# Engine lists ordered with changes of the PE array's tiling counted, and denser fill products in planned gaps

## The chip, the cores and the metric

The kernel runs on one core of a Trainium2 chip. The metric is the device time of one execution in microseconds (us), the median over several runs. Five engines work side by side, each through its own list of instructions in order: PE (TensorE, matmul), ACT (ScalarE), DVE (VectorE), POOL (GpSimd) and SP (SyncE, which here only issues DMA transfers). They wait for one another through semaphores.

## What is computed

The reference, cut to what matters (batch 8, 8 heads, 576 rows of width 64, 32 packed rows, d_ff 2048):

```python
def sm_attn(qq, kk, vv):
    s = scale * np.matmul(qq, kk.transpose(0, 1, 3, 2))
    a = softmax(s)
    return np.matmul(a, vv)
p_packed = sm_attn(p, k, v)             # 32 packed rows attend to 576 rows
out = sm_attn(q, p_packed, p_packed)    # 576 rows attend to the 32 packed ones
x = out.transpose(0, 2, 1, 3).reshape(4608, 512)
h = x @ w_in                            # 512 -> 2048
g = h * (1.0 / (1.0 + np.exp(-beta * h)))
return g @ w_out                        # 2048 -> 512
```

All inputs and the output are float32; the kernel computes its products in bf16.

## The kernel before

Each of the eight batches is one unit of work `b`. 512 of its 576 rows are the main part, the other 64 the "rest", and two batches share one 128-row tile for the last product of the rests.

Attention of a batch: k and q are transposed (by PE for the first two batches, tasks `tr` and `trr`; by DMA from batch 2 on), the scores of the packed rows are products of k and p (`s1`, `s1r`), their exponentials are summed (`z1`) and multiplied with v (`pun`), and DVE normalizes the result to `pp`. Then `s2` makes the scores of the q rows, and `z2` the sums over them. Instead of multiplying the second attention's output with w_in, the kernel first multiplies `pp` with w_in (`w`, product tiles `w_ps`; DVE scales them with beta to `W_bf`), so that one product of `W_bf` with the attention weights `A2T` gives the hidden layer (`h`, sixteen per batch; `hr` for the rests). ACT applies silu (`g`), and the last product (`o`, or for the main part of batches 2 to 7 the seven products `p`/`P` of a Strassen-like scheme with sums `S`, `T4`) goes to the output. The tasks `take`, `add` and `R..` read the product tiles, and `store` writes them out.

`s2` and `w` use the PE array as eight 64x32 tiles at once (eight matmuls with a tile position each, called a burst below); `z1` uses it as two 128x64 tiles. Everything else uses the whole 128x128 array. In the profile all products stand at line 380 (the helper `mm`) and all PE transposes at line 385 (`tp`), so they are told apart by their tiles: `w_ps<-w_in_bf,pp` is `w`, `s_ps<-qT,pp` and `s2r_ps` are the two parts of `s2`, `z_ps<-E1T,ones` is `z1`, `h_ps` is `h`, `pT_ps<-identr,p_dup` is `p_tr`.

The packed rows p of batches 2 to 7 are loaded once (`("ld", "p")`, 384 KB). Two copies, `("p_dup", 0)` and `("p_dup", 1)`, double them into one bf16 tile (line 1168), PE transposes that tile in two halves (`("p_tr", 0)` and `("p_tr", 1)`), each of which reads both copies, and the tasks `pT1` place the result, which the `s1` of batches 2 to 7 read.

The order of every engine's work is written out: `SEQUENCE` holds one list of tasks per engine. `Planner.run` walks the lists, each in its order, with the costs of its tasks (the number or table handed to `task`), and emits the instructions. It emits them in the order of the lists whatever the costs say; two things depend on its times: where ACT's table loads stand in the program, and the fill products. `begin` gives the earliest start of an engine's next task, and `fill` puts fill products (`keep_warm`: 128x128 products of the identity, tile `o_ps<-identr`) into PE's list where `begin` finds a gap before the next task, as long as the time is before `WARM_UNTIL = 60.0` and an output bank is free. A loose task (a conversion) can stand in the list of any of the engines that its cost table names, and the engine is the one in whose list it stands.

PSUM tiles come from rings: four banks `att` for attention and `w` products, two `h`, two `o`. A task that takes a bank waits until the one that held it has been read.

Of the kernel before, what the change touches and what calls it, by code (L numbers as in the profile page):

```python
# [37 lines left out]
WARM_US = 0.3  # L38
# [5 lines left out]
HALVED = (0,)  # L44
PORT = ("S", "T4", "A2", "cast", "w_in", "w_out", "p_dup", "p0_bf")
# [8 lines left out]
        ("brow", 0), ("tr", 0, "k", 0), ("p0_tr", 0), ("brow", 1), ("tr", 0, "k", 1), ("tr", 0, "q", 0),  # L54
        ("trr", 0, "k"), ("brow", 2), ("s1r", 0), ("s1", 0, 0), ("s1", 0, 1), ("brow", 3), ("tr", 0, "q", 1),
        ("p0_tr", 1), ("z1", 0), ("pun", 0, 0), ("pun", 0), ("bcol",), ("s2", 0, 0), ("z2", 0, 0), ("z2", 0, 1),
        ("w", 0, 0), ("w", 0, 1), ("h", 0, 3), ("h", 0, 0), ("tr", 1, "k", 0), ("h", 0, 2), ("h", 0, 1),
        ("tr", 1, "k", 1), ("h", 0, 4), ("o", 0, 0, 1), ("o", 0, 1, 1), ("h", 0, 7), ("h", 0, 6), ("trr", 0, "q"),
        ("w", 0, 2), ("trr", 1, "k"), ("h", 0, 5), ("o", 0, 1, 3), ("o", 0, 0, 3), ("s1r", 1), ("s1", 1, 0),
        ("h", 0, 8), ("h", 0, 9), ("o", 0, 0, 5), ("o", 0, 1, 5), ("s1", 1, 1), ("o", 0, 0, 7), ("o", 0, 1, 7),  # L60
        ("h", 0, 11), ("o", 0, 2, 1), ("w", 0, 3), ("z1", 1), ("o", 0, 2, 3), ("tr", 1, "q", 0), ("o", 0, 2, 5),
        ("h", 0, 10), ("h", 0, 12), ("o", 0, 3, 1), ("h", 0, 14), ("pun", 1, 0), ("o", 0, 2, 7), ("pun", 1),
        ("h", 0, 15), ("h", 0, 13), ("tr", 1, "q", 1), ("o", 0, 3, 3), ("s2", 0, 1), ("o", 0, 3, 5), ("s2", 1, 0),
        ("o", 0, 3, 7), ("w", 1, 0), ("o", 0, 1, 9), ("o", 0, 1, 11), ("o", 0, 0, 9), ("z2", 1, 0), ("o", 0, 0, 11),
        ("z2", 0, 2), ("o", 0, 1, 13), ("trr", 1, "q"), ("o", 0, 1, 15), ("z2", 1, 1), ("o", 0, 0, 13), ("s2", 1, 1),
        ("o", 0, 0, 15), ("o", 0, 2, 9), ("o", 0, 2, 11), ("o", 0, 2, 13), ("z2", 1, 2), ("w", 1, 1), ("o", 0, 3, 9),
        ("o", 0, 3, 11), ("w", 1, 2), ("h", 1, 1), ("h", 1, 3), ("o", 0, 3, 13), ("o", 0, 3, 15), ("h", 1, 0),
        ("w", 1, 3), ("h", 1, 2), ("o", 0, 2, 15), ("p_tr", 0), ("h", 1, 10), ("h", 1, 5), ("p_tr", 1), ("h", 1, 4),
        ("o", 1, 0, 1), ("h", 1, 9), ("o", 1, 1, 1), ("h", 1, 6), ("o", 1, 1, 3), ("h", 1, 8), ("o", 1, 0, 3),
        ("h", 1, 11), ("o", 1, 1, 5), ("h", 1, 7), ("hr", 0, 0), ("o", 1, 0, 5), ("o", 1, 1, 7), ("s1r", 2),  # L70
        ("s1", 2, 1), ("s1", 2, 0), ("o", 1, 1, 9), ("o", 1, 0, 7), ("o", 1, 0, 9), ("hr", 0, 1), ("o", 1, 0, 11),
        ("z1", 2), ("pun", 2, 0), ("pun", 2), ("h", 1, 15), ("o", 1, 1, 11), ("h", 1, 12), ("hr", 1, 0), ("w", 2, 0),
        ("h", 1, 14), ("w", 2, 1), ("h", 1, 13), ("hr", 1, 1), ("w", 2, 2), ("o", 1, 0, 13), ("o", 1, 0, 15),
        ("o", 1, 1, 13), ("o", 1, 1, 15), ("s2", 2, 0), ("o", 1, 2, 1), ("o", 1, 2, 3), ("o", 1, 2, 5), ("z2", 2, 0),
        ("o", 1, 3, 1), ("z2", 2, 1), ("o", 1, 2, 7), ("o", 1, 3, 3), ("o", 1, 2, 9), ("o", 1, 2, 11), ("s2", 2, 1),
        ("o", 1, 2, 13), ("o", 1, 2, 15), ("o", 1, 3, 5), ("o", 1, 3, 7), ("h", 2, 0), ("h", 2, 6), ("s1r", 3),
        ("s1", 3, 1), ("s1", 3, 0), ("o", 1, 4, 1), ("h", 2, 1), ("o", 1, 3, 9), ("z2", 2, 2), ("o", 1, 3, 11),
        ("h", 2, 5), ("o", 1, 4, 3), ("o", 1, 3, 13), ("o", 1, 4, 5), ("o", 1, 4, 7), ("o", 1, 3, 15), ("z1", 3),
        ("w", 2, 3), ("o", 1, 4, 9), ("o", 1, 4, 11), ("h", 2, 7), ("h", 2, 2), ("pun", 3, 0), ("pun", 3),
        ("h", 2, 10), ("o", 1, 4, 13), ("h", 2, 3), ("o", 1, 4, 15), ("h", 2, 8), ("w", 3, 0), ("h", 2, 15),  # L80
        ("w", 3, 1), ("h", 2, 14), ("p", 2, 1, 0), ("h", 2, 11), ("w", 3, 2), ("h", 2, 12), ("p", 2, 1, 1),
        ("h", 2, 4), ("h", 2, 13), ("w", 3, 3), ("h", 2, 9), ("p", 2, 1, 2), ("P", 2, 1), ("hr", 2, 0),
        ("p", 2, 2, 0), ("hr", 2, 1), ("p", 2, 2, 1), ("s2", 3, 0), ("p", 2, 2, 2), ("P", 2, 2), ("s2", 3, 1),
        ("p", 2, 6, 0), ("p", 2, 6, 1), ("z2", 3, 0), ("p", 2, 5, 0), ("z2", 3, 1), ("p", 2, 5, 1), ("p", 2, 6, 2),
        ("P", 2, 6), ("s1r", 4), ("z2", 3, 2), ("s1", 4, 1), ("p", 2, 5, 2), ("s1", 4, 0), ("P", 2, 5),
        ("p", 2, 7, 0), ("p", 2, 7, 1), ("p", 2, 7, 2), ("p", 2, 3, 0), ("p", 2, 3, 1), ("h", 3, 15), ("p", 2, 3, 2),
        ("P", 2, 7), ("h", 3, 14), ("h", 3, 1), ("z1", 4), ("pun", 4, 0), ("h", 3, 8), ("pun", 4), ("h", 3, 7),
        ("p", 2, 4, 0), ("h", 3, 0), ("p", 2, 4, 1), ("h", 3, 9), ("P", 2, 3), ("h", 3, 2), ("p", 2, 4, 2),
        ("h", 3, 5), ("w", 4, 0), ("h", 3, 3), ("w", 4, 1), ("h", 3, 11), ("P", 2, 4), ("h", 3, 10), ("w", 4, 2),
        ("h", 3, 4), ("p", 3, 1, 0), ("h", 3, 13), ("h", 3, 6), ("p", 3, 1, 1), ("w", 4, 3), ("h", 3, 12),  # L90
        ("hr", 3, 0), ("p", 3, 1, 2), ("P", 3, 1), ("p", 3, 2, 0), ("s2", 4, 0), ("p", 3, 2, 1), ("p", 3, 2, 2),
        ("P", 3, 2), ("hr", 3, 1), ("z2", 4, 0), ("s2", 4, 1), ("z2", 4, 1), ("p", 3, 6, 0), ("p", 3, 6, 1),
        ("p", 3, 6, 2), ("z2", 4, 2), ("p", 3, 5, 0), ("P", 3, 6), ("p", 3, 5, 1), ("p", 3, 5, 2), ("s1r", 5),
        ("s1", 5, 1), ("p", 3, 7, 0), ("s1", 5, 0), ("p", 3, 7, 1), ("P", 3, 5), ("p", 3, 7, 2), ("P", 3, 7),
        ("h", 4, 13), ("z1", 5), ("p", 3, 3, 0), ("pun", 5, 0), ("pun", 5), ("h", 4, 0), ("h", 4, 8), ("p", 3, 3, 1),
        ("p", 3, 3, 2), ("h", 4, 15), ("h", 4, 2), ("p", 3, 4, 0), ("p", 3, 4, 1), ("h", 4, 10), ("h", 4, 7),
        ("w", 5, 0), ("p", 3, 4, 2), ("h", 4, 11), ("h", 4, 9), ("w", 5, 1), ("P", 3, 3), ("h", 4, 5), ("h", 4, 1),
        ("P", 3, 4), ("w", 5, 2), ("h", 4, 14), ("h", 4, 3), ("w", 5, 3), ("o", 3, 4, 1), ("h", 4, 4), ("h", 4, 6),
        ("o", 3, 4, 3), ("o", 3, 4, 5), ("hr", 4, 0), ("o", 3, 4, 7), ("h", 4, 12), ("o", 3, 4, 9), ("s2", 5, 0),
        ("o", 3, 4, 11), ("o", 3, 4, 13), ("p", 4, 1, 0), ("o", 3, 4, 15), ("p", 4, 1, 1), ("z2", 5, 0),  # L100
        ("p", 4, 1, 2), ("z2", 5, 1), ("s2", 5, 1), ("P", 4, 1), ("hr", 4, 1), ("p", 4, 2, 0), ("p", 4, 2, 1),
        ("p", 4, 2, 2), ("p", 4, 6, 0), ("P", 4, 2), ("p", 4, 6, 1), ("p", 4, 6, 2), ("h", 5, 7), ("h", 5, 11),
        ("p", 4, 5, 0), ("p", 4, 5, 1), ("h", 5, 3), ("h", 5, 13), ("P", 4, 6), ("p", 4, 5, 2), ("h", 5, 1),
        ("z2", 5, 2), ("h", 5, 10), ("s1r", 6), ("s1", 6, 1), ("P", 4, 5), ("p", 4, 7, 0), ("p", 4, 7, 1),
        ("s1", 6, 0), ("p", 4, 7, 2), ("h", 5, 15), ("h", 5, 8), ("p", 4, 3, 0), ("P", 4, 7), ("p", 4, 3, 1),
        ("p", 4, 3, 2), ("P", 4, 3), ("z1", 6), ("pun", 6, 0), ("pun", 6), ("h", 5, 5), ("p", 4, 4, 0), ("h", 5, 9),
        ("p", 4, 4, 1), ("h", 5, 0), ("w", 6, 0), ("hr", 5, 0), ("w", 6, 1), ("h", 5, 14), ("p", 4, 4, 2),
        ("h", 5, 4), ("w", 6, 2), ("h", 5, 2), ("P", 4, 4), ("h", 5, 12), ("w", 6, 3), ("h", 5, 6), ("p", 5, 1, 0),
        ("hr", 5, 1), ("p", 5, 1, 1), ("s2", 6, 0), ("p", 5, 1, 2), ("P", 5, 1), ("p", 5, 2, 0), ("p", 5, 2, 1),
        ("p", 5, 2, 2), ("P", 5, 2), ("z2", 6, 0), ("p", 5, 6, 0), ("s2", 6, 1), ("z2", 6, 1), ("p", 5, 6, 1),  # L110
        ("p", 5, 6, 2), ("P", 5, 6), ("p", 5, 5, 0), ("s1r", 7), ("s1", 7, 0), ("s1", 7, 1), ("p", 5, 5, 1),
        ("z2", 6, 2), ("p", 5, 5, 2), ("P", 5, 5), ("p", 5, 7, 0), ("h", 6, 8), ("h", 6, 14), ("z1", 7),
# [148 lines left out]
class Planner:  # L261
# [14 lines left out]
    def run(self):  # L276
# [3 lines left out]
        free, done = dict(FROM), {e: 0 for e in todo}  # L280
        freed = {}
        held = {"DVE": 0.0, "POOL": 0.0}
        flight, mode, pipe = [], "exp", 0.0

        def begin(e):
            if done[e] == len(todo[e]):
                return None
            t, at = todo[e][done[e]], free[e]
            if e == "ACT" and t.table not in (None, mode):
                at += TABLE_US  # L290
# [1049 lines left out]
```

## Time and profile before

| | us |
|---|---|
| median of 6 runs | 251.63 |
| lowest and highest of them | 251.26, 252.65 |
| the profiled execution's own time | 251.31 |
| its span, first to last instruction | 249.5 |
| PE busy | 235.7 (94%), 2335 matmuls |
| ACT busy | 174.6 (70%) |
| DVE busy | 154.9 (62%) |
| POOL busy | 62.9 (25%) |
| DMA moved | 54.11 MB |

The costliest groups on PE are `h` (256 matmuls, 72.9 us busy) and the parts of the last product (`o_ps<-...`). Because a matmul's recorded duration overlaps with the next one, the busy sums are too high a measure of the array's work; the distance between two starts is the better one. A group in the profile reads: line, engine, operation, output<-inputs, shapes, count, then busy time, mean ns of one, and the idle time just before with what ended most of it. In the timeline the first two columns are the start in us from the span's beginning and the duration of the merged group.

### The profile page before, as it was taken

How to read it: one execution, taken by the hardware profiler on the slowest of the kernel's cores; microseconds unless marked ns; L12 is line 12 of the kernel's file. 1: busy time of each engine (PE TensorE's matmuls, PEld its weight loads, DVE VectorE, ACT ScalarE, POOL GpSimd, SP SyncE). 2: the span in 40 equal slices, each digit the busy share in tenths (PEclk: the TensorE clock that was granted, in tenths of full speed). 3: DMA queues.
4: the chain of work that ended last, by engine and by line, in shares of the span. 5: the costliest groups of instructions: out<-in, count | busy, mean ns of one | idle time of the engine just before them, and what ended most of it. 6: DMA issues, size and time to landing. Idle time of an engine off the chain costs nothing.

```text
span 249.5 us, 5622 instructions
## 1 busy us (share of the span) xinstructions
PE 235.7 (94%) x2335; PEld 148.0 (59%) x2335; DVE 154.9 (62%) x236; ACT 174.6 (70%) x313; POOL 62.9 (25%) x74
## 2 busy tenths in 40 slices
PE   2985999999999999999999999999999999999992
PEld 1972444433564444686578645776587646767970
DVE  5464768988927536884587475844878356723721
ACT  2385789767797887887688767877797659766110
POOL 8312002006742074055501541523305000000000
PEclk9996599999999999999999999999999999999999
DMA  6999999999999999999499999798491631004122
GB/s 198 302 335 334 336 371 313 350 265 280 160 290 193 301 307 298 244 296 301 112 253 242 327 197 282 177 319 183 92 293 31 117 148 45 1 3 168 45 86 82
DMA packets 74825, 54.11 MB, mean 217 GB/s; under 512 B 42688, under 2 KB 68304, under 8 KB 74800
## 3 DMA queue, kind: packets, MB, share of 16 engines
q1 hardware_dynamic: 74496, 53.68, 80.5%
q8 instruction: 18, 0.29, 0.5%
q10 hardware_dynamic: 304, 0.07, 0.2%
q14 instruction: 7, 0.06, 0.1%
HBM read 37.23 MB, written 9.44 MB: 187 GB/s over the span
## 4 chain that ended last, share of the span: by engine, by line
PE 77%; DMA 16%; POOL 2%; SPq 1%; ACT 1%; DVE 1%; issue 0%; POOLq 0%
PE o_ps L380 42%; PE h_ps L380 21%; DMA k<-in_k_dram 13%; PE w_ps L380 3%; PE hr_ps L380 3%; DMA v<-in_v_dram 3%; PE z_ps L380 2%; PE s_ps L380 2%; PE pp_ps L380 2%; POOL k_bf L461 1%; SPq L440 1%; PE kT_ps L385 1%; ACT L395 1%; SPq L1251 0%; ACT E1T L583 0%; POOL p_dup L1168 0%
## 5 line engine op out<-in xcount | busy, mean ns | idle before, releaser
L823 ACT ACTIVATE g_main<-h_ps 128x512 bf16<-128x512 f32 x128 | 72.7, 596 | 34.6 <-PE h_ps L380 34.5
L380 PE MATMUL h_ps<-A2T,W_bf 128*128 128x512 bf16 x256 | 72.9, 388 | 0.5 <-DVE A2T L733 0.5
L380 PEld LDWEIGHTS <-g_main 128*128 128x128 bf16 x608 | 56.7, 98 | 28.0 <-issue 3.5
L380 PE MATMUL o_ps<-w_out_bf,g_main 128*128 128x256 bf16 (+1 forms) x416 | 72.7, 306 | 0.2 <-DVE o_sb L888 0.2
L792 DVE TENSOR_TENSOR W_bf<-w_ps,beta_bc 128x512 bf16<-128x512 f32 x64 | 41.4, 683 | 17.8 <-PE w_ps L380 17.5
L380 PEld LDWEIGHTS <-W_bf 128*128 128x128 bf16 x512 | 32.5, 99 | 21.8 <-issue 6.6
L395 ACT ACT_TABLE_LOAD x24 | 30.8, 1283 | 1.1 <-PEq L1324 0.7
L380 PE MATMUL o_ps<-w_sum,g_main 128*128 128x256 bf16 x192 | 26.5, 273 | 0.0
L380 PE MATMUL o_ps<-w_sum,g_sum 128*128 128x256 bf16 x192 | 24.7, 273 | 0.0
L461 POOL CAST q_bf<-q 128x1024 bf16<-128x1024 f32 x14 | 16.8, 1206 | 29.5 <-DMA q<-in_q_dram 28.2
L1039 DVE TENSOR_TENSOR o_sb<-o_ps,o_sb 128x512 f32<-128x512 f32 x18 | 12.4, 686 | 16.6 <-PE o_ps L380 15.6
L461 POOL CAST v_bf<-v 128x1024 bf16<-128x1024 f32 x12 | 13.0, 1095 | 33.8 <-DMA v<-in_v_dram 24.5
L380 PEld LDWEIGHTS <-g_sum 128*128 128x128 bf16 x192 | 18.3, 98 | 3.4
L461 POOL CAST k_bf<-k 128x1024 bf16<-128x1024 f32 x12 | 13.2, 1125 | 24.4 <-DMA k<-in_k_dram 23.7
L380 PE MATMUL o_ps<-w_out_bf,g_rem 128*128 128x512 bf16 x64 | 16.8, 380 | 0.0
L380 PEld LDWEIGHTS <-pp 64*32 64x32 bf16 x384 | 5.6, 89 | 18.6 <-issue 15.3
L380 PE MATMUL w_ps<-w_in_bf,pp 64*32 64x512 bf16 x256 | 13.9, 393 | 2.4 <-DVE w_in_bf L1247 1.5
L1041 DVE COPY o_sb<-o_ps 128x512 f32<-128x512 f32 x13 | 9.0, 690 | 10.2 <-PE o_ps L380 10.2
L1009 DVE TENSOR_TENSOR g_sum<-g_main 128x2048 bf16<-128x2048 bf16 x6 | 7.3, 1222 | 10.4 <-ACT g_main L823 10.4
L733 DVE TENSOR_TENSOR A2T<-E2T,rz 128x512 bf16<-128x512 bf16 x16 | 12.2, 776 | 2.5 <-ACT rz L728 2.3
L843 ACT ACTIVATE g_rem<-hr_ps 128x512 bf16<-128x512 f32 x16 | 9.5, 597 | 5.5 <-PE hr_ps L380 5.4
L716 ACT ACTIVATE rz<-z_ps 128x512 f32<-128x512 f32 x16 | 9.5, 593 | 2.1 <-PE z_ps L380 2.0
(102 smaller groups left out, 262.5 us busy)
## 6 DMA issues: line engine op xcount, KB each, us to landing
out_dram<-o_sb SPq DMA_DIRECT2D x14, 512.0 KB, 3.8
k<-in_k_dram SPq DMA_DIRECT2D x6, 1024.0 KB, 8.7
v<-in_v_dram SPq DMA_DIRECT2D x6, 1024.0 KB, 7.7
q<-in_q_dram SPq DMA_DIRECT2D x6, 1024.0 KB, 8.9
w_in<-in_moe_w_in_dram SPq DMA_DIRECT2D x4, 1024.0 KB, 9.9
w_out<-in_moe_w_out_dram SPq DMA_DIRECT2D x4, 1024.0 KB, 10.6
k<-in_k_dram SPq DMA_DIRECT2D x4, 512.0 KB, 9.0
q<-in_q_dram SPq DMA_DIRECT2D x4, 512.0 KB, 7.4
```

What stands on the lines that cost most here:

```text
L380: return self.nc.tensor.matmul(out, lhsT, rhs, start=start, stop=stop, tile_position=pos, skip_group_check=True)
L385: return self.nc.tensor.matmul(out, in_, ident, is_transpose=True, skip_group_check=True)
L395: self.nc.scalar.preload_act_table_set(SETS[mode])
L461: self.copy[engine](o[:, 0:2048].rearrange("p (t h d) -> p h t d", t=4, h=8)[:, h], t[:, 0:2048].rearrange("p (h t d) -> p h t d", h=8, t= ...
L716: nc.scalar.activation(st[b, "rz2"][:, i], ps[:], AF.Ln)
L733: nc.vector.tensor_tensor(part(st[b, "A2"], i), part(st[b, "E2"], i), st[b, "rz2"][:, i] if i < 2 else st[b, "rz2r"][:], ALU.mult)
L792: nc.vector.tensor_tensor(st[b, "W"][:, r, cols], st[b, "w", m][:], self.beta_bc[:, cols], ALU.mult)
L823: nc.scalar.activation(st[b, "g"][:, ft, :], st[b, "h", ft][:], AF.Silu)
L843: nc.scalar.activation(st[b // 2, "gr"][:, 8 * half : 8 * half + 8, o : o + 64], st[b, "hr", half][:].rearrange("p (f n) -> p f n", f=8), ...
L1009: nc.vector.tensor_tensor(o, x, y, op)
L1039: nc.vector.tensor_tensor(o, x, o, ALU.add)
L1041: self.copy[engine](o, x)
```

## The change

The change replaces all five lists of `SEQUENCE` and adjusts costs in the planner. No task is added or removed; PE has 549 tasks before and after. The planner now knows a tiling per kind of task and adds 0.095 us to PE's start where it changes:

```diff
-WARM_US = 0.3
+WARM_US = 0.1
...
+TILED = {"w": 1, "s2": 1, "z1": 2}
+TILED_US = 0.095
...
+            if e == "PE" and TILED.get(t.key[0], 0) != tiled:
+                at += TILED_US
...
-            for _ in range(int((min(at, WARM_UNTIL) - free["PE"]) / WARM_US)):
+            for _ in range(int((min(at - 0.1, WARM_UNTIL) - free["PE"]) / WARM_US)):
                 self.filler()
...
             if e == "PE":
                 fill(at)
+                tiled = TILED.get(t.key[0], 0)
```

Costs of tasks change with it (`w` 0.35 to 0.245, `s2` 0.3 to 0.245 and its rest 0.14 to 0.06, `b_safe` on POOL 1.5 to 2.3, `p0_bf` on POOL 0.6 to 1.0, `T4` 1.15 to 1.25, conversions by 0.02 to 0.06). They act only through the fill products and the table loads. The new lists, in the stretches that matter here. PE, batch 4's products and small-tile bursts:

```diff
-("w", 4, 0), ("h", 3, 3), ("w", 4, 1), ("h", 3, 11), ("P", 2, 4), ("h", 3, 10), ("w", 4, 2),
-("h", 3, 4), ("p", 3, 1, 0), ("h", 3, 13), ("h", 3, 6), ("p", 3, 1, 1), ("w", 4, 3),
+("w", 4, 0), ("w", 4, 1), ("h", 3, 10), ("h", 3, 3), ("p", 2, 4, 0), ("p", 2, 4, 1), ("h", 3, 6),
+("h", 3, 9), ("p", 2, 4, 2), ("P", 2, 4), ("h", 3, 2), ("w", 4, 2), ("w", 4, 3),
```

PE, from the first product that needs the last two loads of w_out (`("o", 0, 1, 13)`) to the first `p_tr`:

```diff
-("o", 0, 1, 13), ("trr", 1, "q"), ("o", 0, 1, 15), ("z2", 1, 1), ("o", 0, 0, 13), ("s2", 1, 1),
-("o", 0, 0, 15), ("o", 0, 2, 9), ("o", 0, 2, 11), ("o", 0, 2, 13), ("z2", 1, 2), ("w", 1, 1),
-("o", 0, 3, 9), ("o", 0, 3, 11), ("w", 1, 2), ("h", 1, 1), ("h", 1, 3), ("o", 0, 3, 13),
-("o", 0, 3, 15), ("h", 1, 0), ("w", 1, 3), ("h", 1, 2), ("o", 0, 2, 15), ("p_tr", 0),
+("o", 0, 1, 13), ("trr", 1, "q"), ("o", 0, 1, 15), ("o", 0, 0, 13), ("s2", 1, 1), ("o", 0, 0, 15),
+("o", 0, 3, 9), ("o", 0, 3, 11), ("z2", 1, 2), ("w", 1, 1), ("o", 0, 3, 13), ("w", 1, 2), ("h", 1, 2),
+("o", 0, 2, 9), ("h", 1, 3), ("o", 0, 3, 15), ("h", 1, 1), ("p_tr", 1), ("h", 1, 0), ("p_tr", 0),
```

The path of p on SP and POOL (before, `("p_dup", 1)` stood in ACT's list, between `g` of batch 1):

```diff
 SP
-("ld", 1, "q", 2), ("ld", 2, "k", 0), ("ld", "p"), ("ld", 2, "v", 0), ("ld", 2, "k", 2),
+("ld", 1, "q", 2), ("ld", "p"), ("ld", 2, "k", 0), ("ld", 2, "k", 2), ("ld", 2, "q", 0),
 POOL
-("w_in", 3, 1), ("cast", 2, "k", 0), ("cast", 2, "k", 1), ("p_dup", 0), ("cast", 2, "k", 2),
+("cast", 1, "q", 2), ("p_dup", 0), ("cast", 2, "k", 0), ("p_dup", 1), ("cast", 2, "k", 2),
```

The start, in short: on SP batch 1's k now comes ahead of the first load of w_out, and the first p ahead of the second half of k; `b_safe` moves from POOL to DVE, both `p0_bf` and the conversions of the second w_in block to POOL, those of the first to DVE, and ACT takes the first piece of batch 0's k and v and of batch 1's k:

```diff
 ACT
-("n2", 0, 1), ("cast", 0, "q", 2), ("w_out", 0), ("g", 0, 0), ("g", 0, 3), ("w_out", 2),
+("n2", 0, 1), ("n2", 0, 0), ("cast", 1, "k", 0), ("g", 0, 0), ("g", 0, 1), ("g", 0, 5),
 DVE
-("w_in", 1, 0), ("w_in", 1, 1), ("A2", 0, 0), ("W", 0, 0), ("W", 0, 1), ("A2", 0, 1),
+("w_in", 0, 1), ("w_in", 0, 0), ("W", 0, 0), ("W", 0, 1), ("beta", 3), ("cast", 0, "q", 2), ("A2", 0, 0),
```

The built program has 119 fill products in place of 38, and as many table loads on ACT as before, 24.

## The prediction

> **What bounds the kernel now.** I read the 40 slices of the page first, then the windows by stage, then the waits of PE, the chain of waits in order of time, and last the timeline of PE around the operations that the change moves.
>
> ```profile
> PE   2985999999999999999999999999999999999992
> PEclk9996599999999999999999999999999999999999
> DMA  6999999999999999999499999798491631004122
> ...
> 50.00:60.00 10.00, 9.79 (x73) 3.75 (x71) 8.91 (x16) 7.80 (x17) 3.01 (x3) 1.00 1.10 264
> 70.00:90.00 20.00, 20.00 (x206) 9.94 (x205) 9.71 (x15) 17.12 (x32) 4.97 (x6) 1.00 1.06 272
> ```
>
> From 70 us on PE is busy without a gap (20.00 of 20.00), and PE's last matmul ends the kernel but for one copy and a store. So what counts after that point is the sum of PE's work. Up to 60 us the picture is another: the DMA share is full (1.10), PE has small waits and, in slices 5 and 6, a lowered clock. There the order in which data land sets the pace. The point where the one regime hands over to the other is in the chain of waits:
>
> ```profile
> 43.28 13.56 DMA k<-in_k_dram
> ...
> 56.99 3.02 POOL k_bf L461 x2
> 60.00 0.99 POOL p_dup L1168
> 61.00 0.05 issue
> 61.04 0.51 PE pT_ps L385 x8
> ```
>
> The load of batch 2's keys lands at 57 us, GpSimd converts it in two pieces (3.02 us), then doubles p (`p_dup`), and only then may PE transpose p (`p_tr`, 61.04). After it the chain is PE to the end. PE stood 0.29 us there: the pair before it took 0.72 us (60.32 to 61.04) where a pair takes 0.43.
>
> The next two stretches price a change of the array's tiling: start us, duration, operation.
>
> ```profile
> 96.04 0.59 PE L380 MATMUL h_ps<-A2T,W_bf 128*128 128x512 bf16 x2
> 96.57 0.41 PE L380 MATMUL w_ps<-w_in_bf,pp 64*32 64x512 bf16 x8
> 96.91 0.61 PE L380 MATMUL h_ps<-A2T,W_bf 128*128 128x512 bf16 x2
> ...
> 203.34 1.03 PE L380 MATMUL h_ps<-A2T,W_bf 128*128 128x512 bf16 x4
> 204.20 0.59 PE L380 MATMUL o_ps<-w_out_bf,g_rem 128*128 128x512 bf16 x2
> 204.72 0.41 PE L380 MATMUL s_ps<-qT,pp 64*32 64x512 bf16 x8
> 204.95 0.21 PE L380 MATMUL s2r_ps<-qT,pp 64*32 64x64 bf16 x8
> 205.10 1.04 PE L380 MATMUL h_ps<-A2T,W_bf 128*128 128x512 bf16 x4
> ```
>
> Matmuls overlap, so I use the distance of starts. A full-array pair takes 0.43 (203.34 to 204.20 is two of them). Ahead of a small-tile burst it takes 0.53 (96.04 to 96.57): 0.10 is lost going in. A lone burst of eight takes 0.34 (96.57 to 96.91), but only 0.23 where another burst of the same 64*32 tiling follows (204.72 to 204.95): 0.11 is lost coming out. So one burst that joins its neighbour saves 0.21 us, 0.105 for each change of tiling.
>
> [...] Here it was lowered from about 21 to 31 us (clock digits 6 and 5), after a stretch in which PE was not idle but busy about a third of the time by its starts. [...] The landings that the trace shows keep the order of issue. [...] The two k conversions took 1.51 us each, lone ones 1.04.
>
> **The change part by part.**
>
> *Fewer changes of tiling.* Counting along PE's list (w and s2 are one tiling, z1 another, all else the full array) gives 106 changes before and 82 after; fillers split one pair in each, so 108 and 84. 24 changes at 0.105 are 2.5 us. All lie in the saturated part, and PE's other work is the same set of tasks.
>
> *Where p_tr stands in PE's list.* This I take to decide how much of that arrives. After the first p_tr the old list has 108 h, 64 o, 24 w and 81 changes; the new one has 109 h, 67 o, 25 w and 58 changes, and the rest of the kinds is equal. So the new list has to do after this point 1 h + 3 o = 4 x 0.43 = 1.72 and 1 w = 0.23 more, and 23 x 0.105 = 2.42 less: 0.47 us less in all. The other 2 us of the gain are spent before p_tr: the new list reaches it sooner.
>
> *When PE reaches it.* Both lists wait for the last two loads of w_out just before. In the trace the o pair with w_out rows 12 and 13 ends at 52.19, held up 0.30 us, and p_tr follows 8.85 us later. In the new list 3 o, 1 h, 1 w (0.44 with its changes) and 1 z2 (0.22) of that stretch are gone: 1.72 + 0.44 + 0.22 = 2.4. PE would arrive at 52.19 + 8.85 - 2.4 = 58.6.
>
> *When p is ready.* SP now issues the load of p ahead of batch 2's k instead of behind it; GpSimd does p_dup 0, the first k piece, p_dup 1 (before, ScalarE did p_dup 1 and GpSimd both k pieces ahead of p_dup 0). p_dup 1 is thus queued behind a conversion that waits for k. k now has 0.39 MB of p ahead of it: at 264 GB/s 1.5 us, so it lands between 57.0 (p runs beside it) and 58.5; I take 58.3. Then a k piece 1.04 (up to 1.51) and p_dup 1.04, with hops 0.1: 60.5, from 59.1 to 61.1. PE waits 60.5 - 58.6 = 1.9 us, and starts p_tr 61.04 - 60.5 = 0.54 sooner than before.
>
> *Other moves before 60 us*: b_safe to VectorE, both p0_bf to GpSimd, the w_in conversions exchanged, batch 1's k ahead of w_out on SP, 119 fillers in place of 38. On ScalarE and VectorE conversions now wait for a load ahead of work that needs none (batch 1's first k piece ahead of the first silu, the q rest ahead of A2). I price all this at nothing: the 1.9 us of PE's wait at p_tr cover it. If the cover is gone, the fillers are the largest term: 81 more at 0.06 to 0.12 (twelve took 1.46 us at the start) are 5 to 10 us of PE time, but each stands in a gap planned at 0.1 us or more, so I bound what sticks out at 0 to 1.5 us.
>
> *Pairs of w after 60 us.* A joined pair fills the four PSUM banks of the attention ring; VectorE empties them at 0.6 us each (W groups of two take 1.28). Between a pair and the next user of the ring the new list has 3 to 4 us of full-array work, and 2.4 us are needed. I take 0, at most 0.2 a pair, 1.2 for six.
>
> Sum: 0.47 + 0.54 = 1.0 us less. The profiled run took 251.31 (span 249.5, 1.8 around it): 250.3. The median of the six runs is 0.3 higher, 251.63, and I forecast on its footing: **250.6**.
>
> **The rivals.**
>
> *The whole gain arrives.* If p is ready by 58.6, nothing holds PE there, and the next limit is the last w_out load: after that o pair the new list is shorter by 25 changes (2.6 us) and some 0.3 of work. For it: DMA order is my estimate, not a reading. Against: the chain shows p_tr bound already, and no landing in the trace can give 58.6 with two GpSimd steps behind k. 251.63 - 2.6 = 249.0, at best 248.3.
>
> *A tie.* The pairs of w and the late conversions give back what is left: 1.0 less 1.0, 251.6.
>
> *Slower: the clock falls.* [...] Price: the lowered stretch before lasted 10 us; with dense work a stretch of half clock costs half its length[...]. [...] The denser fillers work against it earlier, but the list has none at p_tr.
>
> **How the numbers follow.** My forecast 0.55, the whole gain 0.21, the tie 0.10, the fallen clock 0.14. A difference under 0.3% (0.75 us) can't be told from no change. The forecast's own range is 249.2 to 251.2 (ready times 59.1 to 61.1); about three quarters of it is beyond 0.75 us. Faster: 0.41 + 0.21 = 0.62. Within: 0.14 + 0.08 = 0.22. Slower: 0.14 + 0.02 = 0.16. The range 248.3 to 252.4 takes in the whole gain and the tie and leaves the fallen clock out.
>
> **What would show it.** Right: a wait of PE at pT_ps of 1 to 2.5 us, released by GpSimd's p_dup, near 58 to 61 us; joined w bursts of 0.23 us; PE without gaps from there on, its last matmul near 244.0 (245.0 before). Wrong: p_tr without a wait (then the whole gain), a lowered clock after 31 us, gaps of PE at w_ps, or a burst in a pair that still takes 0.34.

## The result and the profile after

| | before | after |
|---|---|---|
| median, us (runs) | 251.91 (68) | 250.55 (31) |
| lowest to highest, us | 250.43 to 253.74 | 248.52 to 251.99 |
| profiled execution, us | 251.31 | 250.93 |
| first `p_tr` starts, us | 61.04 | 60.78 |
| last matmul of PE ends, us | 245.01 | 244.66 |

The ratio of after to before is 0.994, 95% interval 0.9926 to 0.9954: 1.4 us faster, and 250.55 where 250.6 was forecast. The forecast was 1.0 us under a median of 251.63 from six runs; with 68 runs that median is 251.91, so the fall is 1.36 us. The two profiled executions are only 0.4 us apart; runs of one kernel differ by more than 3 us, so a single profile shows where time lies but not the median.

The page of the kernel after, busy tenths in 40 slices:

```profile
PE   4995969979999999999999999999999999999992
PEclk9999999999999999999999999999999999999998
DMA  6999999999999999999999998995860420304024
```

The windows of the kernel after (us, then PE, PEld, DVE, ACT and POOL busy, clock, DMA share, GB/s):

```profile
50.00:60.00 10.00, 8.68 (x67) 3.34 (x66) 8.12 (x17) 6.70 (x15) 2.74 (x4) 1.00 1.10 259
70.00:90.00 20.00, 20.00 (x236) 10.09 (x236) 10.45 (x18) 17.47 (x31) 4.94 (x6) 1.00 1.09 268
180.00:200.00 20.00, 19.54 (x205) 14.01 (x209) 14.35 (x19) 15.33 (x30) 6.62 (x6) 1.00 0.37 94
```

The last of these stretches in the kernel before:

```profile
180.00:200.00 20.00, 20.00 (x226) 14.39 (x225) 13.10 (x18) 15.03 (x29) 3.36 (x3) 1.00 0.64 155
```

In this execution the lowered clock is gone (1.00 from 20 to 30 us, before 0.55), PE is busy for less of the 10 us ahead of `p_tr` (8.68, before 9.79), and from 180 to 200 us it is no longer full (19.54, before 20.00): the first sign of a new wait late in the kernel. The waits of PE (tile, line, released by: us in total, times, longest) name it and the others:

```profile
PE o_ps L383 <- DVE bones L1107: 3.7, 1, 3.7
PE o_ps L383 <- DVE w_out_bf L1261: 2.0, 3, 1.3
PE krT_ps L388 <- DVE k_bf L474: 1.8, 1, 1.8
PE w_ps L383 <- DVE w_in_bf L1250: 1.7, 1, 1.7
...
PE h_ps L383 <- DVE A2T L736: 0.2, 1, 0.2
PE o_ps L383 <- DVE o_sb L1044: 0.2, 1, 0.2
```

The first is a wait of the fill products at the very start. The next three lie ahead of `p_tr`: PE waits for DVE's conversion of data that have just been loaded. The chain of waits of the kernel after, around `p_tr` (start us, us, what):

```profile
45.33 13.22 DMA k<-in_k_dram
...
58.70 0.67 POOL k_bf L464
...
59.69 1.05 POOL p_dup L1171
60.74 0.05 issue
60.78 0.51 PE pT_ps L388 x8
```

k lands at 58.6, POOL converts its first piece, then copies p a second time, and PE transposes: the path that the prediction drew. After it the chain is again PE almost to the end.

### The profile page after: what moved, and what is told of

The parts are those of the page before. It is cut to its first block, busy times and chain, and to the rows that moved or that the text cites. A ratio compares the mean times of both kernels' runs of the same rounds, so it can differ in the third digit from the quotient of the medians.

```text
span 249.2 us, 5792 instructions
## 1 busy us (share of the span) xinstructions
PE 233.0 (94%) x2416; PEld 150.0 (60%) x2416; DVE 156.5 (63%) x235; ACT 175.6 (70%) x312; POOL 64.6 (26%) x76
## 4 chain that ended last, share of the span: by engine, by line
PE 74%; DMA 15%; DVE 4%; ACT 2%; SPq 2%; POOL 1%; issue 1%; POOLq 0%; ACTq 0%
PE o_ps L383 41%; PE h_ps L383 19%; DMA k<-in_k_dram 10%; DMA v<-in_v_dram 4%; PE hr_ps L383 3%; PE w_ps L383 3%; PE z_ps L383 2%; PE s_ps L383 2%; SPq L435 2%; PE pp_ps L383 1%; DVE A2T L736 1%; DMA out_dram<-o_sb 1%; DVE identr L1103 1%; PE brow_ps L383 1%; ACT g_main L826 1%
## 5 line engine op out<-in xcount | busy, mean ns | idle before, releaser
L383 PEld LDWEIGHTS <-g_main 128*128 128x128 bf16 x608 | 56.8, 98 | 29.7 <-issue 5.6
L383 PE MATMUL h_ps<-A2T,W_bf 128*128 128x512 bf16 x256 | 71.3, 380 | 0.4 <-DVE A2T L736 0.2
L464 POOL CAST v_bf<-v 128x1024 bf16<-128x1024 f32 x13 | 17.5, 1357 | 34.3 <-DMA v<-in_v_dram 33.4
L464 POOL CAST q_bf<-q 128x1024 bf16<-128x1024 f32 x14 | 15.4, 1106 | 32.7 <-DMA q<-in_q_dram 14.7
L736 DVE TENSOR_TENSOR A2T<-E2T,rz 128x512 bf16<-128x512 bf16 x16 | 14.7, 937 | 5.1 <-ACT rz L731 5.1
L383 PE MATMUL o_ps<-w_out_bf,g_rem 128*128 128x512 bf16 x64 | 16.9, 379 | 0.0
L464 POOL CAST k_bf<-k 128x1024 bf16<-128x1024 f32 x13 | 14.5, 1123 | 9.5 <-DMA k<-in_k_dram 7.8
L383 PE MATMUL o_ps<-identr 128*128 128x128 bf16 x119 | 10.6, 252 | 3.7 <-DVE bones L1107 3.7
L383 PE MATMUL w_ps<-w_in_bf,pp 64*32 64x512 bf16 x256 | 11.4, 383 | 2.3 <-DVE w_in_bf L1250 1.7
L1044 ACT COPY o_sb<-o_ps 128x512 f32<-128x512 f32 x12 | 7.0, 583 | 9.1 <-PE o_ps L383 9.1
L383 PEld LDWEIGHTS <-pp 64*32 64x32 bf16 x384 | 4.3, 88 | 12.8 <-issue 8.8
L383 PEld LDWEIGHTS <-identr 128*128 128x128 bf16 x119 | 9.0, 115 | 4.8 <-DVE bones L1107 3.7
```

The lines of the kernel that those rows point to most:

```text
L383: return self.nc.tensor.matmul(out, lhsT, rhs, start=start, stop=stop, tile_position=pos, skip_group_check=True)
L464: self.copy[engine](o[:, 0:2048].rearrange("p (t h d) -> p h t d", t=4, h=8)[:, h], t[:, 0:2048].rearrange("p (h t d) -> p h t d", h=8, t= ...
L736: nc.vector.tensor_tensor(part(st[b, "A2"], i), part(st[b, "E2"], i), st[b, "rz2"][:, i] if i < 2 else st[b, "rz2r"][:], ALU.mult)
L1044: self.copy[engine](o, x)
```

## The experiments

In the table, the floor from `p_tr` is the distance from the first `p_tr` to the end of the last matmul less the waits in it (the distance between two starts compared with the median for matmuls of the same kind). "Stalls" are those waits, all of them near 105, 138 or 189 us except one at 75 us. All PE numbers are of one profiled execution each; medians and ratios are over the runs.

| kernel | median us | ratio to before, 95% | `p_tr` at | `p_tr` to end | stalls | floor |
|---|---|---|---|---|---|---|
| before | 251.91 | | 61.04 | 183.96 | small | |
| after | 250.55 | 0.994 (0.9926 to 0.9954) | 60.78 | 183.88 | 1.06 | 182.8 |
| before_join | 250.79 | 0.9957 (0.9934 to 0.9981) | 60.51 | 182.96 | 1.17 | 181.8 |
| after_split | 252.22 | 1.0012 (0.9994 to 1.003) | 60.30 | 186.32 | 1.34 | 185.0 |
| after_p | 250.13 | 0.9933 (0.9913 to 0.9954) | 59.30 | 184.36 | 1.55 | 182.8 |
| after_thin | 249.30 | 0.9901 (0.9874 to 0.9929) | 59.58 | 182.83 | 0 | 182.8 |
| after_rep | 250.56 | 0.994 (0.9917 to 0.9962) | 59.89 | 184.41 | 1.60 | 182.8 |
| after_q | 249.94 | 0.9905 (0.9871 to 0.9938) | 60.57 | 184.20 | 1.34 | 182.9 |
| before_fill | 252.39 | 1.002 (0.999 to 1.0051) | 61.21 | 184.19 | small | |
| after_nofill | 249.18 | 0.9895 (0.9854 to 0.9935) | 59.53 | 185.00 | 2.21 | 182.8 |
| after_qv | 248.57 | 0.9854 (0.9821 to 0.9887) | 60.26 | 182.84 | 0 | 182.8 |
| nofill_qv | 247.92 | 0.983 (0.98 to 0.986) | 57.92 | 182.81 | 0 | 182.8 |
| best | 248.15 | 0.984 (0.9807 to 0.9874) | 59.51 | 183.52 | 0.71 | 182.8 |
| startfill_qv | 248.93 | 0.9859 (0.9825 to 0.9892) | 59.98 | 182.81 | 0 | 182.8 |

Every kernel with the new PE list has nearly the same floor, 182.8 to 182.9 us; only after_split, which alters that list, has another. What differs is when `p_tr` starts, and the stalls.

**Is a change of tiling worth 0.105 us?** Joins alone in the kernel before, and joins undone in the kernel after:

```diff
 PE, before_join (ten such pairs, batches 2 to 7)
-("w", 4, 0), ("h", 3, 3), ("w", 4, 1),
+("w", 4, 0), ("w", 4, 1), ("h", 3, 3),
 PE, after_split (nine such pairs)
-("w", 4, 2), ("w", 4, 3), ("h", 3, 4),
+("w", 4, 2), ("h", 3, 4), ("w", 4, 3),
```

> The kernel before, with ten w bursts of batches 2 to 7 moved in PE's list so that they stand in pairs; all of them lie after the first p_tr, and nothing else is touched. My theory (a joined burst saves 0.21 us wherever PE is the bound; what the change gives before p_tr is taken back by landings): 20 changes of tiling at 0.105 are 2.1 us, so 2.1 us under the kernel before, ratio 0.992, and p_tr starts where it did, near 61 us. Rival 1 (joined bursts give their gain back in new waits for the attention banks): between 0 and 1 us. Rival 2 (the change's gain comes from the denser fill products and the start, not from the tiling): no difference, ratio 1.000.

> The changed kernel, with its nine w pairs of batches 2 to 7 split again: the second burst is moved one product down PE's list. All after p_tr. My theory: 18 changes at 0.105, 1.9 us over the changed kernel, so about 252.4, 0.5 us over the kernel before, ratio near 1.002. Rival 1 (waits): under 1 us over the changed kernel, ratio 0.995 to 0.998. Rival 2 (start and fills): equal to the changed kernel, ratio 0.994.

The same w bursts of batch 4 in the timelines of PE (start us, us, operation), first in the kernel after, then in after_split:

```profile
119.04 0.63 PE L383 MATMUL w_ps<-w_in_bf,pp 64*32 64x512 bf16 x16
119.60 1.04 PE L383 MATMUL h_ps<-A2T,W_bf 128*128 128x512 bf16 x4
```

```profile
119.02 0.41 PE L382 MATMUL w_ps<-w_in_bf,pp 64*32 64x512 bf16 x8
119.37 0.61 PE L382 MATMUL h_ps<-A2T,W_bf 128*128 128x512 bf16 x2
119.90 0.41 PE L382 MATMUL w_ps<-w_in_bf,pp 64*32 64x512 bf16 x8
120.24 0.60 PE L382 MATMUL h_ps<-A2T,W_bf 128*128 128x512 bf16 x2
```

A joined pair takes 0.558 us from its start to the next operation's, a lone burst 0.342, and each entry costs 0.093 in the matmul ahead. So a join saves 2 x 0.342 - 0.558 + 0.093 = 0.22 us. Nine splits should cost 1.97 us; the floor rose by 2.2, and the median by 1.67 us. Here the price per change holds.

In before_join ten joins should save 2.2 us, but the distance from `p_tr` to the end shrank by only 1.00, and the median by 1.1; the 2.1 us (ratio 0.992) that I expected lie outside the interval. The rest went into two new waits, of which the larger is in PE's timeline of before_join, with DVE's beside it:

```profile
105.46 0.22 PE L379 MATMUL s2r_ps<-qT,pp 64*32 64x64 bf16 x8
106.37 0.83 PE L379 MATMUL o_ps<-w_sum,g_sum 128*128 128x256 bf16 x6 [0.68 <-DVE g_sum L1008]
```

```profile
102.05 1.87 DVE L791 TENSOR_TENSOR W_bf<-w_ps,beta_bc 128x512 bf16<-128x512 f32 x3
103.84 1.21 DVE L1008 TENSOR_TENSOR g_sum<-g_main 128x2048 bf16<-128x2048 bf16 x1
105.09 1.22 DVE L1008 TENSOR_TENSOR g_sum<-g_sum,g_main 128x2048 bf16<-128x2048 bf16 x1
```

Two joined w bursts give DVE three scalings in a row (1.87 us; in the kernel before two, 1.29 us) ahead of the sums that the last product needs; the second sum ends at 106.3 (before, 105.5) and PE, which now comes sooner, stands 0.75 us by its starts. The other wait is 0.42 us at 75.4, for a silu of ACT. 2.2 - 0.75 - 0.42 = 1.0, as measured. So part of the gain went back in new waits, though not in those for the attention banks that my rival named. Joins alone are not free; a new list has to move what follows them on DVE as well.

**Does `p_dup` 1 behind k hold PE?**

```diff
 POOL
-("p_dup", 0), ("cast", 2, "k", 0), ("p_dup", 1),
+("p_dup", 0), ("p_dup", 1), ("cast", 2, "k", 0),
```

> The changed kernel, with the second doubling of p directly behind the first in GpSimd's list, ahead of the conversion that waits for batch 2's keys. My theory: p is ready near 56 to 57 us in place of 60.7, PE no longer waits at p_tr, but it is still held by the last load of w_out, so only the 0.3 us that it stood there in the trace comes back: 0.2 to 0.6 us under the changed kernel, ratio 0.992 to 0.993. Rival (the path of p is the one limit ahead of the saturated part): 1.5 us or more under it, ratio 0.988 or lower. Rival 2 (the limit is the landing of w_out alone): no difference from the changed kernel.

250.13 against 250.55, intervals overlapping: at most the small gain expected. `p_tr` moved to 59.30, where nothing holds it. The chain of waits there no longer leads to k but to the last load of w_out, which lands at 51.14 and which DVE then converts ahead of other work that PE needs: the limit that the expectation named.

**Do the fillers cost anything?** Three kernels with other numbers of fill products: after_thin 35, after_nofill none, before_fill 118 in the kernel before (the profile's count; the expectation's 83 was an undercount).

```diff
 after_thin
-WARM_US = 0.1
+WARM_US = 0.3
 after_nofill
-WARM_UNTIL = 60.0
+WARM_UNTIL = 0.0
 before_fill
-WARM_US = 0.3
+WARM_US = 0.1
-            for _ in range(int((min(at, WARM_UNTIL) - free["PE"]) / WARM_US)):
+            for _ in range(int((min(at - 0.1, WARM_UNTIL) - free["PE"]) / WARM_US)):
```

> The changed kernel with the old spacing of fill products (0.3 us of gap for each in place of 0.1): 35 in place of 119. My theory: PE's start lies behind the landings, so the fills are worth nothing on the end: within 0.3 us of the changed kernel, ratio 0.993 to 0.995, though the clock is lowered again somewhere before 31 us. Rival (the gain comes from the clock that the denser fills hold up): 1 us or more slower than the changed kernel, ratio 0.998 or higher.

> The kernel before with only the fill part of the change (83 fillers planned in its gaps, WARM_US 0.1 and 0.1 us held back). Theory A (the loads set p_tr, so what PE does in its gaps ahead of it costs nothing): ratio to before 0.998 to 1.002, no lowered clock at 21 to 31 us, p_tr within 0.5 us of 61.0. Theory B (each filler delays the real matmul behind it, as the faster run with fewer fillers suggests): slower by about 1 us, ratio 1.003 to 1.006, with PE standing less but arriving later at the matmuls ahead of p_tr.

> The changed kernel without any planned filler. Theory A (the loads set p_tr): lowered clock in part of the first 40 us, and still within 0.4 us of the changed kernel, because the slower matmuls lie in waits on loads. Theory B (fillers cost time): faster than the changed kernel by 1.2 us or more, ratio to before at most 0.990. Theory C (the clock decides, and it falls for longer than in the kernel before): slower than the changed kernel by 1 us or more, with lowered clock reaching past 40 us.

> The changed kernel as it is, beside the other three of this call, so that they are compared on one chip. Expected: 0.994 of the time before (0.992 to 0.996), p_tr near 60.8 us or a little earlier, PE about 184 us from p_tr to its last matmul, with 0.8 us of waits near 189 us behind the two slow A2T multiplications. If p_tr comes near 59.5 us here, as it did in the run with fewer fillers, then that run's gain ahead of p_tr was a difference between executions and not the fillers.

I had first expected no difference. The kernel after with few fillers is 1.25 us faster than with all, without any 1.38 us faster, and the kernel before with many 0.46 us slower. The intervals of each pair still touch, but all three point one way. after_rep repeats the median of the kernel after, 250.56; its `p_tr` at 59.89, where the first profile had 60.78, shows how far one execution lies from another and leaves open whether `p_tr` at 59.58 in after_thin was more than that. Theory C, the clock, is out: after_nofill has one slice of lowered clock (digit 8; 0.83 from 20 to 30 us) and is the faster. One rival is left here: the profile of after_thin has no stall and that of after_nofill the largest, so the medians may also differ by how often a run meets the stalls. The next section removes them.

**The stall at 189 us.** The timeline of the kernel after:

```profile
186.10 2.06 POOL L464 CAST v_bf<-v 128x1024 bf16<-128x1024 f32 x1 [19.06 <-DMA v<-in_v_dram]
...
187.18 2.96 DVE L736 TENSOR_TENSOR A2T<-E2T,rz 128x512 bf16<-128x512 bf16 x2
...
188.11 1.49 POOL L464 CAST q_bf<-q 128x1024 bf16<-128x1024 f32 x1
...
189.58 0.38 PE L383 MATMUL h_ps<-A2T,W_bf 128*128 128x512 bf16 x1
...
190.20 0.38 PE L383 MATMUL h_ps<-A2T,W_bf 128*128 128x512 bf16 x1 [0.24 <-DVE A2T L736]
```

The kernel before at the same place:

```profile
187.16 1.28 DVE L733 TENSOR_TENSOR A2T<-E2T,rz 128x512 bf16<-128x512 bf16 x2
...
189.16 1.03 PE L380 MATMUL h_ps<-A2T,W_bf 128*128 128x512 bf16 x4
189.22 1.04 POOL L461 CAST q_bf<-q 128x1024 bf16<-128x1024 f32 x1 [12.19 <-DMA q<-in_q_dram]
```

The new lists let three big POOL casts of batch 7 fall beside the two multiplications for `A2T`; these take 2.3 times as long (the pair 2.96 us beside casts, 1.28 alone), the casts 1.4 to 2 times (1.49 and 2.06 us, alone 1.04), and PE stands 0.79 us by its starts. The other profiles show the same: in all fourteen, each such multiplication with no POOL instruction beside it took 0.67 to 0.69 us (136 of them), and those with casts beside them took up to 1.53. Loads and stores are no rival cause: in the kernel after the DMA digit of that slice (186.9 to 193.1 us) is 0. First I moved the q casts, then the load of v as well:

```diff
 POOL, after_q and after_qv
-("cast", 7, "v", 0), ("cast", 7, "q", 0), ("cast", 7, "v", 1), ("cast", 7, "q", 2), ("cast", 7, "q", 1),
+("cast", 7, "q", 0), ("cast", 7, "q", 1), ("cast", 7, "v", 0), ("cast", 7, "v", 1), ("cast", 7, "q", 2),
 SP, after_qv alone
-("store", 8), ("store", 3, 4), ("tr", 7, "k", 0), ("store", 9), ("ld", 7, "q", 2), ("ld", 7, "v", 0),
+("ld", 7, "v", 0), ("store", 8), ("store", 3, 4), ("tr", 7, "k", 0), ("store", 9), ("ld", 7, "q", 2),
```

> The changed kernel with the two big q casts of batch 7 ahead of v's first one on POOL, so that they run near 170 us in POOL's idle 19 us and not at 188 to 192 us beside DVE's A2T multiplications. Theory (part of the missing gain is lost there, because DVE's multiplication of two bf16 SBUF tiles and POOL's casts keep each other waiting): A2T at 187 us near 1.3 to 2.1 us instead of 2.96, PE's waits at 189 to 191 us (0.24 + 0.22 shown, 0.79 by start to start) gone, PE from p_tr to the end 183.1 instead of 183.9 us, time 0.5 to 0.8 us under the changed kernel. Rival (A2T is late because rz or E2T is, and the casts only lie beside it): A2T still ends at 190.1 us, time unchanged.

> The changed kernel with v's load of batch 7 issued four entries earlier on SP (ahead of store 8, near 168 us instead of 179 us) and the two big q casts ahead of v's on POOL, so that all four big casts run near 171 to 177 us and none beside the A2T multiplications at 187 us. Expected: A2T there 1.28 us, the waits at 189 to 191 us gone, PE 183.1 us from p_tr to the end, 0.6 to 0.8 us under the changed kernel (ratio to before near 0.991). If A2T is still slow with no cast beside it, the casts were not its cause.

after_q is 0.6 us faster in the median (the intervals overlap), but its trace shows that the edit did not do what I meant: the q casts run at 170.71, the two v casts still at 185.89 to 188.9, and the stall is there (0.98 us). The median alone would have passed for a hit. after_qv clears the place; its timeline:

```profile
186.39 1.28 DVE L735 TENSOR_TENSOR A2T<-E2T,rz 128x512 bf16<-128x512 bf16 x2
...
188.80 0.59 PE L382 MATMUL h_ps<-A2T,W_bf 128*128 128x512 bf16 x2
```

A2T takes 1.28 us again, although DMA is now busy there (digit 7), PE has no stall from `p_tr` to the end, and the ratio falls to 0.9854 (0.9821 to 0.9887), clear of the kernel after. That is 2 us in the medians, more than the 1.06 us that the profile of the kernel after shows; profiles with these lists, whatever their fillers and the order of `p_dup`, show stalls of 0 to 2.2 us, so a typical run may well lose more than the profiled one. That part is not shown. Nor is the smaller stall at 138.8, which this edit does not touch and which is absent here: in the kernel after an A2T multiplication took 0.95 us beside a cast 4 us ahead of it, here 0.69.

**Where the fillers cost.** On the lists of after_qv, which have no stall:

```diff
 nofill_qv and best
-WARM_UNTIL = 60.0
+WARM_UNTIL = 0.0
 best besides, on POOL
-("p_dup", 0), ("cast", 2, "k", 0), ("p_dup", 1),
+("p_dup", 0), ("p_dup", 1), ("cast", 2, "k", 0),
 startfill_qv
-WARM_UNTIL = 60.0
+WARM_UNTIL = 8.5
```

> The same, without planned fillers. It tells where the 1.2 us lie by which the changed kernel is faster with few or no fillers. If ahead of p_tr (loads land earlier, p_tr near 59.5 us): 0.8 to 1.2 us under the kernel with the same lists and all fillers. If without fillers only the A2T stall at 187 us is met less often: equal to that kernel within 0.3 us.

> The same, without fillers and with the second p_dup cast directly behind the first on POOL, so that p waits for no k load. Expected: p_tr set by PE at 59.0 to 59.5 us, 0 to 0.5 us under the kernel without that, 248.2 us in all, ratio to before 0.985 to 0.988.

> The changed lists with the earlier v load and q casts, and fillers only at the start (41 ahead of PE's first real work, where PE is idle anyway; none in the gaps after it). In the profiles so far, with all 119 fillers PE's first instruction fetch by DMA (a 16 KB packet that holds one DMA engine for 1.1 us) comes at 13.6 to 15.7 us and SP's issue of the w_in load [...] at 20.1 to 20.8 us; with 35 or none, the fetch at 18.2 to 18.7 us and that issue at 19.1 to 19.7 us. Theory F (the fetch, drawn ahead by the fillers' instructions, delays the w_in load that is then in flight): fetch near 15 to 16.5 us, that issue at 20 us or later, PE's p_tr near 60. Theory O (the fillers in the gaps keep PE busy when a real matmul could start): first fetch earlier all the same, but the issue at 19.1 to 19.7 us as without fillers, p_tr near 59 or sooner. Time 247.9 to 248.6 us, which can hardly tell them apart.

nofill_qv is 0.65 us under after_qv and best 0.42 (intervals overlapping), so where no stall is in play the cost of the fillers is smaller and not clear of the noise. best does not improve on nofill_qv: in its profile the last load of w_out lands at 51.50 (50.26 in nofill_qv) and heads the chain of waits up to `p_tr`. If the fillers cost time, it is ahead of `p_tr`: in the four profiles with no or 35 fillers it starts at 57.92 to 59.58, in five with all fillers and `p_dup` in place at 59.89 to 60.78. The earliest place where they part is DVE's conversion of w_in. Its timeline in after_nofill, in the kernel after and in startfill_qv:

```profile
17.76 1.29 DVE L1250 CAST w_in_bf<-w_in 128x1024 bf16<-128x1024 f32 x2 [0.16 <-DMA w_in<-in_moe_w_in_dram]
```

```profile
19.46 0.69 DVE L1250 CAST w_in_bf<-w_in 128x1024 bf16<-128x1024 f32 x1 [1.45 <-DMA w_in<-in_moe_w_in_dram]
```

```profile
19.36 1.29 DVE L1249 CAST w_in_bf<-w_in 128x1024 bf16<-128x1024 f32 x2 [2.14 <-DMA w_in<-in_moe_w_in_dram]
```

In the last two the load itself lands later. What comes before its landing is a packet of the instruction queue. The view of DMA queues of startfill_qv, from 16.5 to 18 us (packets, MB, share of 16 engines):

```profile
q8 instruction: 1, 0.02, 4.7%
```

4.7% of 16 engines over 1.5 us is 1.1 us of one engine. In after_nofill the same window has none; the packet comes at 18.45, once w_in is in. The queue of the kernel after moves 0.31 MB in 19 packets, 16 KB each; without fillers there are 18. In the traces of the kernels before and after, the first packet starts when PE has begun 286 and 283 of its weight loads and matmuls, and each further one 249 of them later in the mean, so I take the packets for PE's. Each filler is two of these instructions (119 weight loads and 119 matmuls of the identity in the kernel after), so with fillers PE comes to its next packet sooner, here at a time when the DMA share is full (1.05 from 14 to 20 us). startfill_qv has fillers only where PE is idle in any case, and its w_in is late all the same (the issue of the next w_in load at 20.68; 19.08 in after_nofill). That speaks for theory F and against theory O, though its fetch came at 16.9, later than I expected. All eleven profiles that share these start lists agree: in the seven whose first fetch starts at 13.6 to 16.9 us, this load of w_in lands at 18.8 to 19.4; in the four where it starts at 18.2 to 18.7, at 17.3 to 17.9. The load is issued at 8.9 to 9.4 us in all of them. That the two share a DMA engine is not shown, for the trace does not name it.

What is not shown is that these 1.5 us reach the end. At the last load of w_out the two groups already overlap (51.1 to 52.9 against 50.3 to 51.9), and with `p_dup` moved the profile with all fillers has `p_tr` no later (after_p, 59.30) than the one without (best, 59.51). The median of startfill_qv, 248.93, is nearer to after_qv than to nofill_qv, but settles nothing by itself.

## Why the prediction came out right, point by point

- **24 changes at 0.105.** Right, though 23 of them and not all lie behind `p_tr`. From 62 us on the separate stretches of small tiles fell from 40 to 29, and a join saves 0.22 us, which is 0.11 per change.
- **After `p_tr`, 0.47 us less.** The sum was right as far as it went. It left out two things. Small waits of the old list went as well (0.16 at 73.3 and 0.17 at 112.2), which is about half of what the new floor, 182.8, lies under the 183.5 that was implied (183.96 - 0.47); the other half is not accounted for. And 1.06 us of new stalls at 138.8 and 189 us took their place. Together the stretch shrank by 0.08 us in the profile. The step that was priced wrong is "Pairs of w after 60 us ... I take 0" and that nothing else after 60 us was priced: PE's last matmul ended at 244.66, not near 244.0. What came was not a wait at w_ps but, at 189 us, a collision of POOL's casts with DVE.
- **`p_tr` 0.54 us sooner.** It came 0.26 sooner in the profiled execution, because k landed at 58.6 and not at 58.3. (The loads of k and p landed in the order of their issue in both kernels: k at 56.8 and p at 58.5 before, p at 55.0 and k at 58.6 after.) The order of steps and their durations (1.04, 1.05) were as drawn.
- **PE arrives at 58.6 and waits 1.9 us.** Wrong in place, right in effect. PE came at 60.48 and stood 0.3 us, so the sign that was named for being right, a wait of 1 to 2.5 us for `p_dup`, did not show. The work that the new list leaves out ahead of `p_tr` was as drawn. What failed is that both lists meet the last w_out loads at the same time: the pair with rows 12 and 13 ended at 54.4, not 52.19, since the load landed 2 us later (52.9, before 50.9), and PE waited 1.31 us there. It is the same cover, one load earlier: what PE saves ahead of 60 us ends in a wait for DMA.
- **Other moves before 60 us at nothing.** Not confirmed for the fillers. Their bound of 0 to 1.5 us holds what the runs show (0.4 to 1.4), but the mechanism named, fillers sticking out of their gaps, is not what the traces point to.
- **The rivals.** The whole gain did not arrive, but the path of p was the smaller reason: freeing it (after_p) gave 0.4 us, within the noise, while moving the casts (after_qv) gave 2 us and brought the fall to 3.7 us (ratio 0.9854), more than the 2.6 to 3.3 that the rival named. The clock did not fall (digit 9 in every slice but the last, which has 8), and that was worth nothing that could be seen. With all fillers it stood at 1.00 from 20 to 30 us, with none at 0.83 (after_nofill). How empty a stretch must be for it to fall is not shown by these runs, so the price and the chance of that rival were the author's estimates. (The lowered digits of the kernel before are the fourth and fifth slice, not "5 and 6"; the 21 to 31 us are right.)

That the forecast was met within 0.1 us owes much to luck. In the two profiles PE's last matmul ends only 0.35 us sooner, where 1.0 was worked out: a gain that was not priced (0.7 in the floor) and two losses (1.06 in stalls, 0.28 at `p_tr`) partly cancel. The median fell by 1.36 us. The other 1.0 us of that is the distance of the two profiled executions from their medians, 0.6 under that of the kernel before and 0.4 over that of the kernel after, and no trace here shows where it lies.

## What to carry to other kernels

When a saturated engine's list is made shorter, look at every other engine's work that was hidden under it: here casts slid beside two-input DVE operations, 0.79 us in one profile, and moving one load and two casts brought back 2 us in the median. Work that only fills gaps need not be free because the gaps are idle: its instructions come by DMA too (here 19 packets of 16 KB with 119 fillers, 18 with none), and here an early fetch went with a load that landed 1.5 us later. And judge an edit by the trace as well as by the time, since after_q's median fell although the edit did not do what it was meant to.

## What the runs showed of the hardware

- A lowered clock cost nothing that could be seen. Among the runs of the kernel after, the nine with a mean clock of 0.982 to 0.988 have a median of 250.55 us, the ten at 0.999 or 1.0 one of 250.45. In the profiles the lowered stretches end by 38.4 us, in the part where loads set the pace, or begin behind PE's last matmul.
- The first packet of the instruction queue (16 KB), taken for PE's, took 1.05 to 1.29 us. In the loaded first 60 us there were four such packets with all fillers and three without.
- Two DVE multiplications of 128x512 bf16 tiles took 1.28 us alone and up to 2.97 us beside POOL casts, while the casts went from 1.04 to 1.5 or 2.1 us.
- The lowest median is that of nofill_qv, 0.983 of the time before (0.98 to 0.986), with the changed lists, no fill products, one load and two casts moved. It can't be told from that of best, 0.984.
